# Three attention steps as one group, with one inserted piece, up to step 237

## The chip, the cores and the metric

The kernel runs on one core of a Trainium2 chip. The metric is the device time of one execution in microseconds. The profile is of one execution; its times are counted from the first instruction of the program.

## The reference

Two kinds of layer follow each other, twice: multi-head attention with a residual, then Fourier mixing (FNet) with a residual, each on a layer-normalised input. The sequence has 2048 rows of 640 columns; there are 32 heads of 20 columns.

```python
def _A_ref(x, wqkv, wo):
    qkv = (x @ wqkv).reshape(B, S, 3, H, Dh) ...
    scores = einsum("bhqd,bhkd->bhqk", q, k) * (Dh ** -0.5)
    o = einsum("bhqk,bhkd->bhqd", softmax(scores), v)
    return o.reshape(B, S, D) @ wo

x = x + _A_ref(_layernorm(x), A_wqkv, A_wo)
x = x + _B_ref(_layernorm(x), ...)      # real part of a two-sided DFT
x = x + _A_ref(_layernorm(x), A_wqkv, A_wo)
x = x + _B_ref(_layernorm(x), ...)
```

## The kernel before

Each of the two layers has four stages: a prologue (loading, normalising, transposing, and the q, k and v of the first heads), attention, the output projection, and the Fourier stage. The change lies in attention.

**Steps.** Attention goes through 512 steps. A step is a group of four heads (`g`, eight of them), a block of 512 queries (`qb`, four) and a block of 128 keys (`kc`, sixteen); `kc` runs innermost. `scores(n, j)` (L477) makes one *score tile* of step n, two heads, j = 0 or 1: two matmuls (L483) into one of three PSUM tiles of two banks each, `p0` to `p2`, taken in turn, and the exp of it on ScalarE (L486) into one of seven SBUF tiles `e0` to `e6`, also in turn. So a score tile can be written only when the exp of the tile three before it has read its PSUM tile, and an exp only when the values have read the tile seven before. `values(n)` (L488) multiplies the four heads' exps of a step with v: four matmuls (L494), each of them two records in the profile, into the accumulator `acc`, one PSUM bank that collects sixteen steps. Then `finish` (L499) transposes it out on VectorE (L501), divides, transposes back, splits it in two parts and stores them with eight DMAs on GpSimd's queue (L515).

**Inserted work.** The q, k and v of the later heads are computed between the steps. `work` (L347) is a generator of *pieces*. A q or k block of 512 columns is a product of fifteen matmuls of 512 columns (L127, tile `pqk`), cut in a piece of eight and one of seven; after the second, `keep` (L209) copies, splits and squares it on VectorE and stores it. Two steps later `after` (L361) makes the *norm product* (L227, tile `pn`), whose maximum VectorE takes (L228). A v block is fifteen matmuls of 320 columns (tile `pv`), again eight and seven. All pieces and norm products share one PSUM bank, `fill`. `due` (L561) says how many pieces should be done by a step, from the marks of L559 (80 at step `THIN`); `need` (L598) forces them where the next head group wants them. In the first layer `compare` (L587) also hands out VectorE work step by step that tests whether the DFT matrices are mirrored (class `Check`, tiles `cq`, `far`).

**Order.** The program is written in the order in which each engine is to work, and that order stands; only semaphores are added. `sweep` (L518) is that order: at each step `begin` (key bounds, tasks, forced pieces), the loads of the next queries and keys on SyncE's queue (L446 to L464), both score tiles, then `between` (L626: `fill`, a piece or a norm product, and then up to two comparisons), then values. Up to step `THIN` = 236 a step with a piece does no values and the next step does all that are owed, so that values go two steps at a time next to pieces and one at a time elsewhere. After it values go one step at a time, or two to catch up after a piece.

`general` (L634) repeats the sweep for inputs whose bound is too loose; it is not taken here.

Of the kernel before, what the change touches and what calls it, by code (L numbers as in the profile page):

```python
# [35 lines left out]
def mha_fnet_kernel(ctx, tc, x_in, wqk, wv, wo, seq, hid, nat_seq, nat_hid, out):  # L36
# [123 lines left out]
    class Qkv:  # L160
# [256 lines left out]


    class Attention:
        THIN = 236  # L420

        def __init__(s, qkv, L):
            s.a = qkv
# [64 lines left out]
        def values(s, n):  # L488
            g, qb, kc = s.steps[n]
            if kc == 0:  # L490
                s.acc = bank("acc", [128, 512], "acc")
            for j in range(4):
                v0 = (4 * g + j) * VW
                PE.matmul(s.acc[32 * j:32 * j + 32], s.a.v[kc][:, v0:v0 + 32], s.e[n, j // 2][:, j % 2],  # L494
                          start=kc == 0, stop=kc == NT - 1, skip_group_check=True)
            if kc == NT - 1:
                s.finish(g, qb)

        def finish(s, g, qb):  # L499
            t0 = s.room("ofsh", [16, 32], F32, "of")  # L500
            V.transpose(t0.rearrange("p b c -> p (b c)"), s.acc)  # L501
            rc = const.tile([128, 16], F32, name="rc", bufs=2)
            V.tensor_scalar(rc, t0[:, :, DH], 1e-30, None, op0=OP.max)
            V.reciprocal(rc, rc)
# [10 lines left out]
                    G.dma_start(s.o[k, h * DH:(h + 1) * DH, qb * 512:(qb + 1) * 512],  # L515
                                hl[k][32 * j:32 * j + DH])

        def sweep(s, shift, begin, fill):  # L518
            done = calm = 0
            for n, (g, qb, kc) in enumerate(s.steps):  # L520
                begin(n, g, qb, kc)
                last = qb == NB - 1
                if kc == (7 if last else 10 if g == LATE else 4) and not (last and g == H // 4 - 1):
                    s.qload(*((g, qb + 1) if not last else (g + 1, 0)), shift)
                if last and g + 1 < H // 4:
                    for f, j in {1: [(0, 0)], 9: [(0, 1)], 11: [(1, 0)]}.get(kc, []):
                        s.kload(g + 1, f, j)
                if qb == 0 and kc == 0 and g:
                    s.kload(g, 1, 1)
                s.scores(n, 0)  # L530
                s.scores(n, 1)

                more, owed = fill(n) and n >= 2 and n + 1 < len(s.steps), n - 1 - done
                if n < s.THIN:
                    if more and kc != 1:
                        continue
                    count = owed
                else:  # L540
                    if more and owed < 3:
                        calm = n + 6
                        continue
                    count = min(owed, 1)
                    if owed > 1 and (done + 1) % NT and n >= calm:
                        calm = n + 6
                        count = 2
                for _ in range(count):
                    s.values(done)
                    done += 1  # L550
            for n in range(done, len(s.steps)):
                s.values(n)

        def run(s, done, project, check):

# [31 lines left out]
            def compare(n):  # L587

                for _ in range(2):
# [8 lines left out]
            def need(n, *keys):  # L598
                while not all(k in s.a.made for k in keys):
                    if s.after:  # L600
                        fill(s.after[0])
# [29 lines left out]
            s.sweep("b", begin, between)  # L631
            assert not s.work and not later and not tasks, (len(later), len(tasks))

        def general(s, project):  # L634

            f = nc.values_load(s.a.flag[0:1, 0:1], min_val=0, max_val=1)
            with tc.If(f < 1):
# [30 lines left out]
                s.sweep("m", lambda *_: None, lambda *_: None)  # L668
                for f in sum(project.early.values(), []):
                    f()  # L670

# [685 lines left out]
```

## Time and profile before

| what | value |
|---|---|
| median of three runs | 2623.97 us (2621.59 to 2625.21) |
| profiled execution, its own time | 2620.62 us |
| its span, first to last instruction | 2618.8 us |
| first attention, 97.1 to 1149.9 us | 1052.8 us |
| second attention, 1408.3 to 2453.5 us | 1045.2 us |
| exps, one of 128x1024 | 2048, mean 1115 ns with overlap |
| value matmuls (records) | 8192, busy 1062.4 us |
| score matmuls | 4096, busy 815.6 us |

A row of a timeline gives the start, the time from the first start to the last end, the engine, the line and operation, output and input tile, and the number of instructions merged in the row; in brackets stands the idle time before it and what ended it. Starts are measured; ends of matmuls are modelled, and consecutive matmuls overlap. A row of stretches gives the length and the busy time of each engine with the number of its instructions, then the granted TensorE clock, and the DMA share and rate. PE is TensorE's matmuls, PEld its weight loads, DVE is VectorE, ACT ScalarE, POOL GpSimd, SP SyncE.

### The profile page before, as it was taken

The numbers are of one execution on the slowest core, as the hardware profiler recorded it, in microseconds if no ns is written. First come the engines' busy times: TensorE is split into PE (matmuls) and PEld (weight loads), VectorE is DVE, ScalarE is ACT, GpSimd is POOL, SyncE is SP. The second block draws the span as 40 slices with busy tenths as digits, with TensorE's granted clock in tenths as the row PEclk, the third lists the DMA queues.
The fourth block names the chain that finished last, engine by engine and source line by source line (L and its number), as shares of the span: only waits on it lengthen the run. The fifth ranks groups of instructions, "written<-read, shape, count | busy, mean of one in ns | idle before, by whom it ended". The sixth has DMA issues, their size and how long they took to land. (4 is left out here: it accounts for less than half of the span.)

```text
span 2618.8 us, 43736 instructions
## 1 busy us (share of the span) xinstructions
PE 2524.8 (96%) x16350; PEld 1162.1 (44%) x16350; DVE 981.4 (37%) x2079; ACT 2137.4 (82%) x2429; POOL 528.6 (20%) x1068
## 2 busy tenths in 40 slices
PE   7999999999999999999879999999999999999998
PEld 6643444443333332248666444444433333322586
DVE  5355533455444434416652333111321212121265
ACT  5588899988999999964245888999899999999652
POOL 2122111222221122213420111111111111211233
PEclk9999999999999999999989999999999999999998
DMA  4244322333333223326442232111121212132364
GB/s 165 97 127 133 107 94 76 104 99 114 116 112 104 82 60 102 108 83 231 175 175 81 79 100 68 55 28 60 62 73 55 74 41 65 49 89 91 112 232 156
DMA packets 124942, 264.05 MB, mean 101 GB/s; under 512 B 28080, under 2 KB 52432, under 8 KB 124700
## 3 DMA queue, kind: packets, MB, share of 16 engines
q1 hardware_dynamic: 83804, 150.61, 17.5%
q0 software_dynamic: 40896, 110.34, 13.3%
q8 instruction: 137, 2.24, 0.4%
q14 instruction: 105, 0.86, 0.1%
HBM read 176.60 MB, written 84.21 MB: 100 GB/s over the span
## 5 line engine op out<-in xcount | busy, mean ns | idle before, releaser
L486 ACT ACTIVATE e<-psc 128x1024 f32<-128x1024 f32 x2048 | 1938.3, 1115 | 162.9 <-PE psc L483 122.1
L494 PE MATMUL acc<-e,v 128*32 128x512 f32 x8192 | 1062.4, 602 | 7.0 <-DVE of L501 6.4
L483 PE MATMUL psc<-stq,stk 62*128 62x512 f32 x4096 | 815.6, 463 | 3.0 <-ACT e L486 3.0
L483 PEld LDWEIGHTS psc<-stq,stk 62*128 62x128 f32 x4096 | 341.4, 184 | 836.0 <-ACT e L486 781.0
L494 PEld LDWEIGHTS acc<-e,v 128*32 128x32 f32 x8192 | 187.6, 108 | 369.3 <-issue 338.6
L515 POOL DMA_DIRECT2D o<-oh x256 | 131.0, 519 | 941.0 <-DVE oh L510 939.0
L127 PE MATMUL pqk<-xt,wqk 128*128 128x512 f32 x1200 | 314.1, 405 | 6.6 <-DVE top L228 4.8
L127 PEld LDWEIGHTS pqk<-xt,wqk 128*128 128x128 f32 x1200 | 215.4, 188 | 91.3 <-issue 37.9
L501 DVE STREAM_TRANSPOSE of<-acc 128x512 f32<-128x512 f32 x64 | 45.9, 717 | 527.3 <-PE acc L494 527.3
L112 DVE CAST hl<-pqk 128x512 fp32r<-128x512 f32 x64 | 44.2, 691 | 423.2 <-PE pqk L127 419.2
L127 PE MATMUL pv<-wv,xt 128*128 128x320 f32 x960 | 161.3, 318 | 4.3 <-DVE hl L220 4.1
L127 PEld LDWEIGHTS pv<-wv,xt 128*128 128x128 f32 x960 | 142.1, 189 | 31.6 <-issue 24.5
L515 POOL DMA_DIRECT2D o<-ot x256 | 128.3, 508 | 0.7 <-issue 0.4
L120 PE MATMUL py<-wo,o 128*128 128x320 f32 x320 | 100.5, 314 | 14.4 <-DVE xr L904 7.6
L222 POOL DMA_DIRECT2D scrq<-hl x40 | 28.4, 710 | 385.6 <-DVE hl L115 263.7
L721 DVE TENSOR_REDUCE far<-cq 128x1 f32<-128x512 f32 (+5 forms) x169 | 98.6, 584 | 5.7
L121 PE MATMUL py<-wo,o 128*128 128x320 f32 x320 | 99.5, 311 | 0.0
L122 PE MATMUL py<-wo,o 128*128 128x320 f32 x320 | 99.4, 311 | 0.0
L725 DVE TENSOR_TENSOR cq<-cq 128x512 f32<-128x512 f32 (+4 forms) x166 | 96.5, 581 | 3.3 <-DMA cq<-in_nat_seq_dram 3.0
L258 DVE COPY v<-pv 128x320 f32<-128x320 f32 x32 | 15.7, 490 | 182.1 <-PE pv L127 182.1
L222 POOL DMA_DIRECT2D scrk<-hl x40 | 28.1, 702 | 272.4 <-DVE hl L115 244.0
L716 POOL DMA_DIRECT2D cq<-in_nat_seq_dram x64 | 46.3, 729 | 129.5 <-DVE far L721 107.7
(191 smaller groups left out, 1755.7 us busy)
## 6 DMA issues: line engine op xcount, KB each, us to landing
cq<-in_nat_seq_dram POOLq DMA_DIRECT2D x64, 512.0 KB, 5.6
scrq<-hl POOLq DMA_DIRECT2D x40, 512.0 KB, 3.2
scrk<-hl POOLq DMA_DIRECT2D x40, 512.0 KB, 3.4
stq<-scrq SPq DMA_DIRECT2D x256, 80.0 KB
stk<-scrk SPq DMA_DIRECT2D x128, 160.0 KB
o<-o SPq DMA_DIRECT2D x16, 1280.0 KB
stq<-scrq SPq DMA_DIRECT2D x256, 40.0 KB
stk<-scrk SPq DMA_DIRECT2D x128, 80.0 KB
```

The source lines that it names most:

```text
L120: PE.matmul(out_ap, ah, bh, start=start, stop=False)
L121: PE.matmul(out_ap, ah, bl, start=False, stop=False)
L122: PE.matmul(out_ap, al, bh, start=False, stop=stop)
L127: yield lambda i=i, j=j, k=k: PE.matmul(out_ap, a[i], b[j], start=dc == 0 and k == 0, stop=dc == ND - 1 and k == 2)
L222: G.dma_start(s.scr["qk"[k]][c * 128:(c + 1) * 128, :, tb * 512:(tb + 1) * 512], hl.bitcast(F32))
L483: PE.matmul(p[:, i], s.k[g, kc // 8, j][r, kc % 8 * 128:(kc % 8 + 1) * 128], s.q[g, qb, j][r], start=True, stop=True)
L486: A.activation(e, p, AF.Exp, scale=SCALE)
L494: PE.matmul(s.acc[32 * j:32 * j + 32], s.a.v[kc][:, v0:v0 + 32], s.e[n, j // 2][:, j % 2], start=kc == 0, stop=kc == NT - 1, skip_group_ch ...
L515: G.dma_start(s.o[k, h * DH:(h + 1) * DH, qb * 512:(qb + 1) * 512], hl[k][32 * j:32 * j + DH])
L716: G.dma_start(t, quarters[i])
L721: V.tensor_reduce(to, x, op=OP.max, axis=AX.X, apply_absolute_value=True)
L725: V.tensor_tensor(y, x, y, op=op)
```

## The change

Up to step `THIN`, now 237, three steps go together. Scores are still issued in the order of steps. A piece, where one is due, stands between the two score tiles of the steps with `kc` 2, 5, 8, 11 and 15, and behind both of step 13 (there only if no block is half done). Values of all steps before the present one are done in one run behind the scores of the steps with `kc` 0, 3, 6, 9, 12 and 13: three steps each time, and one at 13. The norm product of a block, and up to three comparisons, come behind a value run (`close`). `finish` becomes a generator: its first transpose is issued with the last values, its remainder behind the run and, up to step 237, behind the norm product and the comparisons. After a block's last chunk a pause of four steps is kept where new weights were split. The bound of the next head group and its first key load come one step later. After step 237 the rule for values is what it was, but comparisons now come behind the values and the rest of `finish` instead of before them.

```diff
@@ work()
                             if i + 1 < len(order):
+                                s.pause = 4 if i != 3 else 0
                                 w[i + 1] = s.weights(...)
...
-        THIN = 236
+        THIN = 237
...
             if kc == NT - 1:
-                s.finish(g, qb)
+                s.tail = s.finish(g, qb)
+                next(s.tail)
 
         def finish(s, g, qb):
             t0 = s.room("ofsh", [16, 32], F32, "of")
             V.transpose(t0.rearrange("p b c -> p (b c)"), s.acc)
+            yield
...
-        def sweep(s, shift, begin, fill):
-            done = calm = 0
+        def sweep(s, shift, begin, fill, close):
+            done, calm, s.tail = 0, 0, ()
...
-                    for f, j in {1: [(0, 0)], 9: [(0, 1)], 11: [(1, 0)]}.get(kc, []):
+                    for f, j in {2: [(0, 0)], 9: [(0, 1)], 11: [(1, 0)]}.get(kc, []):
...
                 s.scores(n, 0)
+                if n < s.THIN and kc in (2, 5, 8, 11, NT - 1):
+                    fill(n)
                 s.scores(n, 1)
-                more, owed = fill(n) and n >= 2 and n + 1 < len(s.steps), n - 1 - done
                 if n < s.THIN:
-                    if more and kc != 1:
-                        continue
-                    count = owed
+                    if kc == 13:
+                        fill(n)
+                    if kc in (0, 3, 6, 9, 12, 13):
+                        while done < n:
+                            s.values(done)
+                            done += 1
+                        close(n, 3)
+                        list(s.tail)
+                    continue
+
+                owed = n - 1 - done
+                if fill(n) and owed < 3 and n + 1 < len(s.steps):
+                    calm = n + 6
                 else:
-                    if more and owed < 3:
-                        calm = n + 6
-                        continue
-                    count = min(owed, 1)
-                    if owed > 1 and (done + 1) % NT and n >= calm:
-                        calm = n + 6
-                        count = 2
-                for _ in range(count):
-                    s.values(done)
-                    done += 1
+                    count = 2 if owed > 1 and n >= calm and (done + 1) % NT else min(owed, 1)
+                    if count == 2:
+                        calm = n + 6
+                    for _ in range(count):
+                        s.values(done)
+                        done += 1
+                    list(s.tail)
+                close(n, 2)
...
-                    s.after = (n + 2, f) if f and not s.more else None
-                    s.rest = n + 4 if s.after else n
+                    s.after = (n + (1 if n < s.THIN else 2), f) if f and not s.more else None
+                    s.rest = n + (2 if n < s.THIN or not s.after else 4)
...
+            def after(n):
+                if s.after and n >= s.after[0]:
+                    f, s.after, s.a.pause = s.after[1], None, 0
+                    f()
+                    s.rest = max(s.rest, n + s.a.pause)
+
             def fill(n):
-                if s.after:
-                    if n >= s.after[0]:
-                        f, s.after = s.after[1], None
-                        f()
-                elif s.work and n >= s.rest and (s.more and n < s.THIN or s.blocks < due(n + 1)):
+                if n >= s.THIN:
+                    if s.after:
+                        return after(n)
+                elif s.after or s.more and n % NT == 13:
+                    return
+                if s.work and n >= s.rest and (s.more and n < s.THIN or s.blocks < due(n + 1)):
                     block(n)
-                    s.rest = max(s.rest, n + 2)
                     return s.work
...
-                    when, to = 0, g + 1
+                    when, to = 1, g + 1
...
-            def between(n):
-                more = fill(n)
-                compare(n)
-                return more
+            def close(n, count):
+                if n < s.THIN:
+                    after(n)
+                compare(n, count)
```

More of the change, by code (lines that the diff above doesn't have):

```diff
@@ L530, in sweep @@
                 s.scores(n, 0)
+                if n < s.THIN and kc in (2, 5, 8, 11, NT - 1):
+                    fill(n)
                 s.scores(n, 1)
-                more, owed = fill(n) and n >= 2 and n + 1 < len(s.steps), n - 1 - done
                 if n < s.THIN:
-                    if more and kc != 1:
-                        continue
-                    count = owed
-                else:
-                    if more and owed < 3:
+                    if kc == 13:
[10 more added lines that the diff above has]
+                    calm = n + 6
+                else:
+                    count = 2 if owed > 1 and n >= calm and (done + 1) % NT else min(owed, 1)
+                    if count == 2:
                         calm = n + 6
-                        continue
-                    count = min(owed, 1)
-                    if owed > 1 and (done + 1) % NT and n >= calm:
-                        calm = n + 6
-                        count = 2
-                for _ in range(count):
-                    s.values(done)
-                    done += 1
+                    for _ in range(count):
[3 more added lines that the diff above has]
+                close(n, 2)
             for n in range(done, len(s.steps)):
                 s.values(n)
+            list(s.tail)
         def run(s, done, project, check):
@@ L575, in block, with compare @@
                     tasks.extend(done())
-            def fill(n):
-                if s.after:
-                    if n >= s.after[0]:
-                        f, s.after = s.after[1], None
-                        f()
-                elif s.work and n >= s.rest and (s.more and n < s.THIN or s.blocks < due(n + 1)):
+            def after(n):
[3 more added lines that the diff above has]
+                    s.rest = max(s.rest, n + s.a.pause)
+            def fill(n):
+                if n >= s.THIN:
[4 more added lines that the diff above has]
+                if s.work and n >= s.rest and (s.more and n < s.THIN or s.blocks < due(n + 1)):
                     block(n)
-                    s.rest = max(s.rest, n + 2)
                     return s.work
-            def compare(n):
-                for _ in range(2):
+            def compare(n, count):
+                for _ in range(count):
                     if not later or n < s.landed or (len(check) - len(later)) * 490 >= n * len(check):
@@ L600, in need @@
                     if s.after:
-                        fill(s.after[0])
+                        after(s.after[0])
                     else:
@@ L624, in begin @@
                     f()
-            def between(n):
-                more = fill(n)
-                compare(n)
-                return more
-            s.sweep("b", begin, between)
+            def close(n, count):
+                if n < s.THIN:
+                    after(n)
+                compare(n, count)
+            s.sweep("b", begin, fill, close)
             assert not s.work and not later and not tasks, (len(later), len(tasks))
@@ L667, in general @@
                 s.qload(0, 0, "m")
-                s.sweep("m", lambda *_: None, lambda *_: None)
+                s.sweep("m", lambda *_: None, lambda n: None, lambda *_: None)
                 for f in sum(project.early.values(), []):
```

## The prediction

> **What bounds the kernel now.** I read the page first (busy time by engine, the 40 slices, the costliest groups), then the busy time of each engine over four stretches that I cut at the first score matmul of each attention, at step 237 and at its end, then the order in which TensorE, ScalarE and VectorE start their work inside two short windows. The chain of waits is of little use here: it follows TensorE almost throughout. From the page:
>
> ```profile
> PE 2524.8 (96%) x16350; PEld 1162.1 (44%) x16350; DVE 981.4 (37%) x2079; ACT 2137.4 (82%) x2429; POOL 528.6 (20%) x1068
> ...
> L486 ACT ACTIVATE e<-psc 128x1024 f32<-128x1024 f32 x2048 | 1938.3, 1115 | 162.9 <-PE psc L483 122.1
> ...
> scrq<-hl POOLq DMA_DIRECT2D x40, 512.0 KB, 3.2
> ```
>
> From the stretches (columns: length, then busy time of PE, PEld, DVE, ACT, POOL); the first and third are steps 0 to 236 of the two attentions, and the same stretches for the score line alone show 948 matmuls, that is 237 steps of four:
>
> ```profile
> 97.10:625.65 528.55, 521.30 (x3453) 220.04 (x3452) 250.63 (x508) 459.38 (x475) 105.94 (x181) 1.00 0.34 107
> 625.65:1149.90 524.25, 518.68 (x3429) 165.01 (x3432) 217.17 (x511) 508.27 (x550) 116.45 (x209) 1.00 0.31 95
> 1408.30:1933.35 525.05, 520.91 (x3453) 219.89 (x3452) 136.25 (x250) 459.12 (x475) 75.45 (x140) 1.00 0.21 67
> 1933.35:2453.50 520.15, 517.48 (x3427) 164.78 (x3430) 104.38 (x214) 508.08 (x550) 77.60 (x150) 1.00 0.22 65
> ...
> 97.10:625.65 528.55, 174.24 (x948) 71.93 (x948) 1.00 0.34 107
> 1408.30:1933.35 525.05, 174.06 (x948) 71.79 (x948) 1.00 0.21 67
> ```
>
> The reader is to see two regimes. Up to step 237 TensorE is busy 99% of 528.55 and 525.05 us and ScalarE 87%: TensorE sets the pace. After it ScalarE is busy 97%. But 87% is little room: whatever lets TensorE run ahead meets ScalarE soon. And the granted clock is 1.00 in all four, so it plays no part. What the groups cost TensorE is read as the distance from one start to the next in its timeline (the ends are modelled and overlap):
>
> ```profile
> 303.19 0.73 PE L483 MATMUL psc<-stq,stk 62*128 62x512 f32 x4
> 303.85 0.39 PE L227 MATMUL pn<-sq,ind 128*32 128x512 bf16 x1
> 303.86 1.24 PE L494 MATMUL acc<-e,v 128*32 128x512 f32 x8
> 305.03 0.73 PE L483 MATMUL psc<-stq,stk 62*128 62x512 f32 x4
> ...
> 307.41 2.14 PE L127 MATMUL pqk<-xt,wqk 128*128 128x512 f32 x8
> 309.47 0.73 PE L483 MATMUL psc<-stq,stk 62*128 62x512 f32 x4
> 310.13 1.92 PE L494 MATMUL acc<-e,v 128*32 128x512 f32 x16
> 311.99 0.73 PE L483 MATMUL psc<-stq,stk 62*128 62x512 f32 x4
> 312.65 1.88 PE L127 MATMUL pqk<-xt,wqk 128*128 128x512 f32 x7
> 314.46 0.73 PE L483 MATMUL psc<-stq,stk 62*128 62x512 f32 x4
> ...
> 319.48 1.06 PE L494 MATMUL acc<-e,v 128*32 128x512 f32 x8
> 320.47 0.73 PE L483 MATMUL psc<-stq,stk 62*128 62x512 f32 x4
> 321.13 1.44 PE L127 MATMUL pv<-wv,xt 128*128 128x320 f32 x8
> 322.50 0.74 PE L483 MATMUL psc<-stq,stk 62*128 62x512 f32 x4
> 323.17 1.92 PE L494 MATMUL acc<-e,v 128*32 128x512 f32 x16
> 325.02 0.73 PE L483 MATMUL psc<-stq,stk 62*128 62x512 f32 x4
> 325.69 1.29 PE L127 MATMUL pv<-wv,xt 128*128 128x320 f32 x7
> 326.90 0.74 PE L483 MATMUL psc<-stq,stk 62*128 62x512 f32 x4
> ```
>
> So: scores of one step (two tiles) 0.66; a piece of a q/k block 2.06 (eight matmuls) or 1.81 (seven); of a v block 1.37 or 1.21; values of one step 0.99 (319.48 to 320.47) and of two together 1.86 (each instruction has two records, hence x8 and x16); a norm product 0.19 (1.18 for it and one step of values, less 0.99). I check these prices on the program as it is. Counted in its built order, steps 0 to 236 hold 235 score groups and one of two steps (2.04 from its rows), 76 single and 79 double value runs, 24 norm products, 24 + 24 q/k pieces, 16 + 16 v pieces: 155.1 + 2.0 + 75.2 + 146.9 + 4.6 + 92.8 + 41.3 = **517.9 us**. The stretches took 528.55 and 525.05, so 7 to 11 us are waits, and the prices hold.
>
> **What the change does to TensorE.** The built order of the changed kernel has the same 80 pieces before step 237, one norm product fewer (it comes later, 0.2), and otherwise other groups: 69 cycles of the form *three score tiles, piece, three score tiles, three steps of values*; four with six tiles and no piece; one at the start with five tiles, piece, three tiles; and 14 short groups *two tiles, (piece), one step of values*. Each three steps thus have two score groups and one value run in place of three and about two. The new prices: a third step of values adds 1.86 - 0.99 = 0.87, so 2.73 for three (bounds: 0.87 and 0.99 for that third). A third score tile is read from the window at the start of the first attention, the one place where before issues more than two in a row:
>
> ```profile
> 99.81 0.96 PE L483 MATMUL psc<-stq,stk 62*128 62x512 f32 x6
> 101.43 0.50 PE L483 MATMUL psc<-stq,stk 62*128 62x512 f32 x2 [0.65 <-ACT e L486]
> 101.85 1.89 PE L127 MATMUL pqk<-xt,wqk 128*128 128x512 f32 x7
> ...
> 100.35 3.77 ACT L486 ACTIVATE e<-psc 128x1024 f32<-128x1024 f32 x4 [0.73 <-PE psc L483]
> ```
>
> Six matmuls last 0.96 against 0.73 for four, so a tile adds 0.23 and three tiles cost 0.89. TensorE's work alone would then be 139 x 0.89 + 13.6 + 3.3 (the longer and the short score groups: 4 x 1.58, 1.35, 14 x 0.66 = 16.9) + 74 x 2.73 + 14 x 0.99 + 4.4 + 134.1 = **495 us**, 23 less per attention.
>
> **The wait that it adds.** The same four rows show it. There are three score banks. The fourth tile of that window (101.43) stood 0.65 us for ScalarE: it uses the bank of the first, whose exp began at 100.35, so a bank comes free 1.08 after its exp begins, and the tile that had to wait then takes 0.42 until the next group begins (unhindered the last tile of a group takes 0.33, half of 0.66). The pitch of exps is (3.77 - 1.03) / 3 = 0.913, with one exp's length and its start from:
>
> ```profile
> 324.33 1.02 ACT L486 ACTIVATE e<-psc 128x1024 f32<-128x1024 f32 x1 [0.19 <-PE acc L494]
> 325.62 2.91 ACT L486 ACTIVATE e<-psc 128x1024 f32<-128x1024 f32 x3 [0.27 <-PE psc L483]
> 328.73 1.03 ACT L486 ACTIVATE e<-psc 128x1024 f32<-128x1024 f32 x1 [0.19 <-PE acc L494]
> ```
>
> Scores issued at 325.02 have their exp at 325.62: 0.60. Now one new cycle, tiles A to F, from the start of A:
> - exp of A at 0.60, of C two pitches later, at 2.43.
> - F takes C's bank, free at 2.43 + 1.08 = 3.51. With the eight-matmul q/k piece F would be ready at 0.89 + 2.06 + 0.56 = 3.51, just in time; with 1.81, 1.37, 1.21 or no piece it is ready earlier and stands.
> - the values begin at 3.51 + 0.42 = 3.93, and TensorE is back at A after 3.93 + 2.73 = **6.66 us, whatever the piece**.
> - ScalarE does not run ahead meanwhile: its sixth exp begins at 0.60 + 5 x 0.913 = 5.17 and ends near 6.2, and the next A comes at 6.66, its exp at 7.26. It idles 1.2 us in each cycle, because TensorE, in order, cannot give it scores during 2.73 us of values. The ring of seven exp tiles does not add to this: F's exp waits for the first step of values, released 1.16 after a run begins (323.17 to 324.33), here at 5.09, before 5.17.
>
> Queued behind the waiting F is the value run, and the next scores behind that; who waits is ScalarE. For a rule of TensorEngine Tiling, Performance Considerations (PSUM Bottleneck), in the Trainium skill, that tiling speeds TensorE and not the emptying of PSUM, the trace agrees: by it a cycle stays at 6.66, and without it at TensorE's 5.7 to 6.6.
>
> Per attention: 73 x 6.66 = 486.2; the first cycle 8.7 (fifth tile at 0.60 + 0.913 + 1.08 = 2.59, then 0.42 + 2.06 + 0.89 + 2.73); the short groups 5 x (0.66 + 1.37 + 0.99) + 5 x (0.66 + 2.06 + 0.99) + 4 x 1.65 = 40.3; 23 x 0.19 = 4.4 for norm products. For VectorE I add 3: the norm's reduction now stands just before the next piece, in the one bank of pieces.
>
> ```profile
> 304.28 0.68 DVE L228 TENSOR_REDUCE top<-pn 32x1 f32<-32x512 f32 x1 [1.48 <-PE pn L227]
> ```
>
> It ends 1.11 after the norm (303.85) starts; the piece comes at 0.19 + 0.89 = 1.08 in a long cycle, at 0.85 in the four short ones. The bounds are 1 (no other VectorE work in front) and 12 (one more instruction of 0.68 in front of each of the 17 such pieces). The sum is **542.6 us**, against 528.55 and 525.05: +14.0 and +17.6. Before paid less in the stretches of v pieces: the two-step round 321.13 to 325.69 takes 4.56, 2.28 a step, next to rounds without a piece; 6.66 for three is 2.22 a step in all of them.
>
> **What else moves.** The transpose that frees the accumulator is now issued ahead of the rest of its step's VectorE work, and comparisons (three at each value run, two before at each step) behind it. After step 237 that can help the first attention, which takes 524.25 there against 520.15 in the second, which has no comparisons; I take -2 of these 4.1 (bounds -4 and +2: comparisons that fell behind are caught up there). The moved norm product costs 0.2 each time. The key load one step later, the bound's chain one step later and the output DMAs (same number, issued behind the values) have several steps of lead on SP's and POOL's queues: nothing, and without that cover one landing at each of the seven changes of head group, some 3.2 us by the page's store of a q block.
>
> Sum: 31.6 - 2 + 0.4 = +30. On the profiled execution's 2620.62 this is 2650.6; the median of the runs, 2623.97, lies 3.4 higher, which would give 2654. I forecast **2652 us**.
>
> **Rivals.** *Fewer switches pay.* If F found its bank free (exps keep up, or the 0.42 and 1.08 overlap the piece), the cycles would cost TensorE's work alone: 6.57, 6.32, 5.88, 5.72, and 5.48 (six exps) without a piece; 504.5 us per attention, -44.6 in all, **2578**. For it speaks the page's 96% of PE against 82% of ACT; against it the 0.65 us wait. It decides by whether F stands behind `ACT e`. The Trainium skill's TensorEngine Tiling, Tiling Modes (Key Properties), says a change of tiling mode drains TensorE, and would give this rival; the 0.99 against 0.87 for a step of values agrees in kind. *Half of it*: F stands half as long: 523.6, about **2616**. *Slower than before by more*: with comparisons issued three at a time, one pair (0.68 + 0.69, as below) stands in front of the reduction or of the piece's copies, and 17 pieces of the first attention wait 1.4 us each: +24, **2676**; it decides if the piece's start stands behind `DVE top`.
>
> ```profile
> 309.47 0.69 DVE L721 TENSOR_REDUCE ctop<-cq 128x1 f32<-128x512 f32 x1 [4.51 <-DMA cq<-in_nat_seq_dram]
> 310.07 0.68 DVE L725 TENSOR_TENSOR cq<-cq 128x512 f32<-128x512 f32 x1
> ```
>
> That the grouping does not happen is excluded by the built order.
>
> **How the numbers follow.** Forecast 0.80, switches pay 0.09, half 0.04, VectorE 0.07. The forecast's own bounds: F's 0.42 as 0.33 is -13; the third step of values as 0.99 is +18; VectorE and the part after step 237 -6 to +13; not all at the same end, 2634 to 2676, which takes in the VectorE case and leaves the two faster ones out. Faster by over 0.2% (about what a measurement of this kernel can tell) 0.11, within it 0.04, slower 0.85.
>
> **What would show it.** Steps 0 to 236 take 540 to 546 us in both attentions with ScalarE at 84% or less; three-step rounds last 6.6 to 6.7 us with every kind of piece, the v pieces too; the sixth tile's row names `ACT e`; ScalarE's idle time behind `PE psc` grows from 122 us. I am wrong if rounds with v pieces last under 6.2 us, or if the loss is found after step 237.

## The result: 1.55% slower, where 1.1% was forecast

| | before | after |
|---|---|---|
| median of four runs | 2622.78 us | 2662.70 us (2657.77 to 2666.54) |
| ratio, with its 95% interval | | 1.0155 (1.0129 to 1.0181) |
| span of the profiled execution | 2618.8 us | 2662.9 us |

The forecast was 2652 us, with a range of 2634 to 2676 and 0.85 on slower. The medians lie 40 us apart where the forecast had 28 (30 between executions); the two profiled executions lie 44.1 us apart. From the page of after, the busy time of the engines and the groups of exps and of score matmuls:

```profile
PE 2535.5 (95%) x16350; PEld 1196.7 (45%) x16350; DVE 979.7 (37%) x2079; ACT 2112.0 (79%) x2429; POOL 528.1 (20%) x1068
...
L490 ACT ACTIVATE e<-psc 128x1024 f32<-128x1024 f32 x2048 | 1912.9, 1121 | 233.8 <-PE psc L487 219.0
...
L487 PE MATMUL psc<-stq,stk 62*128 62x512 f32 x4096 | 826.9, 466 | 43.1 <-ACT e L490 37.9
```

The same exps are done, and ScalarE now waits 219.0 us for scores where it waited 122.1. At the same time the score matmuls stand 37.9 us for exps (3.0 before, by the grouped view). Each engine waits for the other more than it did. Where that is, the stretches of after say, cut as those of before (length, busy PE, PEld, DVE, ACT, POOL, then the granted clock):

```profile
97.98:653.30 555.32, 532.53 (x3460) 237.37 (x3460) 248.23 (x505) 446.15 (x474) 104.69 (x179) 0.98 0.31 100
653.30:1174.00 520.70, 516.92 (x3417) 165.70 (x3416) 218.30 (x514) 507.99 (x549) 116.42 (x209) 1.00 0.31 95
1433.20:1978.40 545.20, 522.87 (x3461) 234.23 (x3460) 133.36 (x244) 446.35 (x475) 75.33 (x139) 1.00 0.20 63
1978.40:2499.00 520.60, 517.01 (x3415) 165.60 (x3414) 106.68 (x220) 508.00 (x549) 78.17 (x151) 1.00 0.22 66
```

Against the rows of before, steps 0 to 236 cost 26.8 and 20.2 us more (555.32 for 528.55, 545.20 for 525.05), the first attention's remainder 3.5 less, the second's 0.5 more. So the place is the forecast one: ScalarE's share there falls to 80% and 82%, TensorE's busy time, whose ends are modelled, grows by 11.2 and 2.0, and the loss is in how the two take turns. A whole round with a v piece, with the end of the one before it and the start of the next, on TensorE; then the exps of it and of the one before it, on ScalarE:

```profile
344.33 0.83 PE L487 MATMUL psc<-stq,stk 62*128 62x512 f32 x4
345.58 0.50 PE L487 MATMUL psc<-stq,stk 62*128 62x512 f32 x2 [0.42 <-ACT e L490]
346.01 2.78 PE L498 MATMUL acc<-e,v 128*32 128x512 f32 x24
348.72 0.96 PE L487 MATMUL psc<-stq,stk 62*128 62x512 f32 x6
349.62 1.28 PE L127 MATMUL pv<-wv,xt 128*128 128x320 f32 x7
350.83 0.99 PE L487 MATMUL psc<-stq,stk 62*128 62x512 f32 x4
352.23 0.50 PE L487 MATMUL psc<-stq,stk 62*128 62x512 f32 x2 [0.42 <-ACT e L490]
352.66 2.78 PE L498 MATMUL acc<-e,v 128*32 128x512 f32 x24
355.37 0.73 PE L487 MATMUL psc<-stq,stk 62*128 62x512 f32 x4
```

```profile
342.67 5.61 ACT L490 ACTIVATE e<-psc 128x1024 f32<-128x1024 f32 x6 [1.25 <-PE psc L487]
349.32 5.61 ACT L490 ACTIVATE e<-psc 128x1024 f32<-128x1024 f32 x6 [1.05 <-PE psc L487]
```

The round runs from 348.72 to 355.37: 6.65 us. Its exps begin at 349.32, 0.60 after the scores; the sixth tile (352.23) stands for `ACT e`; the values run from 352.66, and ScalarE, which does six exps in 5.61, had idled 1.05 before it got these scores. This is the cycle that the prediction drew.

The mean rounds of the second attention, by kind, in us:

| round | count | predicted | measured |
|---|---|---|---|
| v piece of eight or of seven | 10 and 16 | 6.66 | 6.66 and 6.68 |
| q/k piece of seven | 24 | 6.66 | 6.58 |
| q/k piece of eight, no norm product | 5 | 6.66 | 6.72 |
| q/k or v piece of eight, with norm product | 13 and 1 | 6.85 | 7.09 and 6.96 |
| no piece (with norm product) | 1 (3) | 6.66 (6.85) | 6.89 (6.96, and one of 8.46) |
| the first one | 1 | 8.7 | 8.64 |
| short, with piece: v; q/k | 5; 1 | 3.02; 3.71 | 3.03; 3.71 |

The table cuts a round at its first matmul, the norm product included. A norm product begins 2.60 after the start of the value run before it, the next scores without one 2.71, so the 24 rounds with a q/k piece of seven, which all end at a norm product, count 0.11 short: to the next scores they last 6.69. Told without that cut, the time from a round's first scores to its values is 3.94 (the median) with every kind of piece, where the prediction had 3.93, and three steps of values take 2.71 where it had 2.73.

One thing was not in the forecast: 0.98 in the clock column of the first attention. Two neighbouring stretches of it, the first from the start of the scores of a round without a piece, the second its values, and the timeline of the same time:

```profile
280.60:285.00 4.40, 3.01 (x16) 1.28 (x12) 1.16 (x3) 4.40 (x5) 1.46 (x2) 0.87 0.51 135
285.00:290.40 5.40, 5.40 (x28) 1.01 (x26) 0.00 (x0) 2.11 (x3) 0.00 (x0) 0.50 0.71 239
```

```profile
281.56 0.50 PE L487 MATMUL psc<-stq,stk 62*128 62x512 f32 x2 [0.21 <-ACT e L490]
282.47 0.50 PE L487 MATMUL psc<-stq,stk 62*128 62x512 f32 x2 [0.41 <-ACT e L490]
283.39 0.56 PE L487 MATMUL psc<-stq,stk 62*128 62x512 f32 x2 [0.42 <-ACT e L490]
284.31 0.86 PE L487 MATMUL psc<-stq,stk 62*128 62x512 f32 x2 [0.35 <-ACT e L490]
285.10 5.35 PE L498 MATMUL acc<-e,v 128*32 128x512 f32 x24
290.38 1.08 PE L487 MATMUL psc<-stq,stk 62*128 62x512 f32 x6
```

Without a piece between them, four score tiles in a row wait for exps. Towards the end of these 4.4 us the granted clock falls (to 0.50, from 283.8 on, for 6.8 us), and the value run behind them takes 5.28 (285.10 to 290.38) instead of 2.72. There are five such groups in each attention, the first round (whose fourth and fifth tile wait, ahead of its piece) and the four rounds without a piece. In the first attention the low clock befell four of them, the first round among them, in the second attention one.

### The profile page after: what moved, and what is told of

Same layout as the page of the kernel before. It is cut to its first block, busy times and chain, and to the rows that moved or that the text cites. A ratio compares the mean times of both kernels' runs of the same rounds, so it can differ in the third digit from the quotient of the medians.

```text
span 2662.9 us, 43748 instructions
## 1 busy us (share of the span) xinstructions
PE 2535.5 (95%) x16350; PEld 1196.7 (45%) x16350; DVE 979.7 (37%) x2079; ACT 2112.0 (79%) x2429; POOL 528.1 (20%) x1068
## 5 line engine op out<-in xcount | busy, mean ns | idle before, releaser
L490 ACT ACTIVATE e<-psc 128x1024 f32<-128x1024 f32 x2048 | 1912.9, 1121 | 233.8 <-PE psc L487 219.0
L498 PE MATMUL acc<-e,v 128*32 128x512 f32 x8192 | 1032.9, 604 | 2.3 <-DVE of L506 1.8
L487 PE MATMUL psc<-stq,stk 62*128 62x512 f32 x4096 | 826.9, 466 | 43.1 <-ACT e L490 37.9
L487 PEld LDWEIGHTS psc<-stq,stk 62*128 62x128 f32 x4096 | 359.2, 184 | 821.9 <-ACT e L490 635.4
L498 PEld LDWEIGHTS acc<-e,v 128*32 128x32 f32 x8192 | 198.2, 109 | 397.9 <-issue 380.6
L736 POOL DMA_DIRECT2D cq<-in_nat_seq_dram x64 | 46.9, 735 | 166.5 <-DVE far L741 135.5
```

The lines of the kernel that those rows point to most:

```text
L487: PE.matmul(p[:, i], s.k[g, kc // 8, j][r, kc % 8 * 128:(kc % 8 + 1) * 128], s.q[g, qb, j][r], start=True, stop=True)
L490: A.activation(e, p, AF.Exp, scale=SCALE)
L736: G.dma_start(t, quarters[i])
```

## Experiments

Four theories stood against each other for the loss. *Bank*: the forecast's cycle, in which the sixth tile waits for a PSUM bank and the long value run for the sixth tile. *Work*: TensorE itself does more or slower work (mode switches, loads of the queries). *Clock*: the excess over the forecast is the low clock in groups without a piece. *Stretch*: what the change loses, it loses next to v pieces, where before paid 2.28 us a step.

**e1, fill the waits.** Matmuls that nobody reads stand where a three-step group has no piece: eight of them, and four in the first group.

```diff
                 if n < s.THIN and kc in (2, 5, 8, 11, NT - 1):
+                    was = s.blocks
                     fill(n)
+                    if shift == "b" and s.blocks == was:
+                        s.idle(8)
+                if n == 1 and shift == "b":
+                    s.idle(4)
```

> The changed kernel, with eight idle matmuls in each group of six score tiles that has no piece, and four behind the third tile of the first group; their product is read by nobody. Clock theory: in the changed kernel these groups leave TensorE mostly waiting for 4.3 us, the granted clock then falls to 0.50 for 3.4 or 6.8 us, and the value run behind takes up to 5.3 us instead of 2.71. With the idle matmuls the clock stays at 1.00 up to step 237, and the six places give back 2.6 + 1.5 + 2.9 + 2.4 us in the first attention and 1.5 in the second: about 11 us less than the changed kernel, some 2651 us; steps 0 to 236 take 546 and 544 us instead of 555.3 and 545.2. Rival: these value runs are slow because the query loads run at the same time (239 GB/s in that stretch); then nothing changes, 2662 us, and the runs still last 4 to 5.3 us.

Median 2656.48 us, ratio to before 1.0125 (1.0109 to 1.0142); the profiled span is 7.5 us shorter than after's. Steps 0 to 236 of the two attentions, and the TensorE timeline around a filled group:

```profile
97.80:645.27 547.47, 529.94 (x3497) 241.24 (x3497) 248.34 (x505) 446.25 (x474) 104.66 (x179) 1.00 0.32 102
...
1426.94:1971.06 544.12, 528.24 (x3497) 239.92 (x3496) 133.34 (x244) 446.68 (x475) 75.33 (x139) 1.00 0.20 63
```

```profile
277.76 2.11 PE L528 MATMUL idle<-xt 128*128 128x512 f32 x8
279.80 0.96 PE L487 MATMUL psc<-stq,stk 62*128 62x512 f32 x6
280.70 2.78 PE L498 MATMUL acc<-e,v 128*32 128x512 f32 x24
283.41 0.97 PE L487 MATMUL psc<-stq,stk 62*128 62x512 f32 x6
```

More work, less time: the value run is back at 2.71 (280.70 to 283.41), the filled rounds last 6.96 to 7.01, but for one of 7.23 and one of 8.38, and the first one 8.73 and 8.65. The first attention gains 7.9 us, the second, which had one low-clock round, 1.1. The DMAs move 348 GB/s during that very run (239 in the stretch of after's), so the rival, that query loads slow these runs, falls and the clock theory holds. The medians differ by 6 us where 11 were expected. One short fall of the clock is left in the steps, at 586.9, behind a wait for VectorE (below); it lies in the round of 8.38.

**e2, give the values back in two runs.** The first two steps of values go ahead of the sixth score tile, the third behind it.

```diff
+                if n < s.THIN and kc in (0, 3, 6, 9, 12):
+                    while done < n - 1:
+                        s.values(done)
+                        done += 1
                 s.scores(n, 1)
```

> The changed kernel, with the value run of three steps split: two steps of values, the sixth score tile, then one step of values. Bank theory: the sixth tile no longer stands for its bank, and ScalarE gets a tile in the middle of the run; a round with a v piece costs 0.89 + 1.37 or 1.21 + 0.66 + 1.86 + 0.43 + 0.99 = 6.2 or 6.0 us instead of 6.66, one with a q/k piece 6.6 or 6.9 instead of 6.6 or 6.75, and the rounds without a piece leave TensorE waiting less, so that the clock falls less often. In all 10 to 30 us less than the changed kernel, 2632 to 2652 us. Rival, switches: each of the 74 rounds of an attention has two groups more at 0.33 us for both, 49 us more in all, about 2711 us.

2649.91 us, ratio 1.0102 (1.0085 to 1.0119), 13 us under after. TensorE has more groups to change between, and yet a round is over sooner; one round with a v piece of eight in the second attention:

```profile
1661.71 0.96 PE L487 MATMUL psc<-stq,stk 62*128 62x512 f32 x6
1662.60 1.43 PE L127 MATMUL pv<-wv,xt 128*128 128x320 f32 x8
1663.97 0.84 PE L487 MATMUL psc<-stq,stk 62*128 62x512 f32 x4
1664.73 1.92 PE L498 MATMUL acc<-e,v 128*32 128x512 f32 x16
1666.59 0.51 PE L487 MATMUL psc<-stq,stk 62*128 62x512 f32 x2
1667.02 1.06 PE L498 MATMUL acc<-e,v 128*32 128x512 f32 x8
1668.02 0.96 PE L487 MATMUL psc<-stq,stk 62*128 62x512 f32 x6
```

From 1661.71 to 1668.02 are 6.31 us in place of 6.66: the sixth tile no longer stands, since its bank comes free while two steps of values run. What remains in this round is work. Rounds with a v piece of seven last 6.30, not the 6.0 that was expected: there the fifth tile still waits a little, and the two kinds come out alike again. That speaks for the bank and against the theory that changes between groups are what costs.

**e3 and e10, a slower ScalarE.** If the bank sets the round, a longer pitch of exps lengthens every round alike. e3 puts one copy of a single column behind each exp of steps 0 to 236, e10 two copies that do not depend on each other (shown).

```diff
             A.activation(e, p, AF.Exp, scale=SCALE)
+            if n < s.THIN and s.short:
+                for x in (zero, one):
+                    A.activation(x, x, AF.Copy)
```

> The changed kernel, with a one-column copy on ScalarE behind each exp before step 237. Its price is bounded by 0.19 us (the accumulator read of before) and 0.39 us (a two-column activation of before). Bank theory: the sixth tile waits for the third exp, two pitches behind the first, so each three-step round grows by two prices, 0.4 to 0.8 us, and 73 rounds of each attention by 28 to 57 us: 2719 to 2776 us, rounds at 7.0 to 7.4 us with every kind of piece. Rival: TensorE's own work sets the 6.66 us (runs of three cost more than their rows say); ScalarE idles 1.2 us in a round, six copies take that up or little more, and the time grows by less than 0.1 us a round at the lower price, under 2677 us.

e3 took 2682.61 us in its one run, far under what the bank theory was expected to give and 6 us above the bound of its rival. The copy is what was mis-sized: it overlaps the exp, and the pitch went only from 0.905 to 0.997. For that pitch the bank's rule (twice the pitch, less the 0.06 by which the first exp then began earlier) gives +0.12 a round, and the rounds grew from 6.66 and 6.68 to 6.78 and 6.80. It agrees, but by too little to settle anything.

> The changed kernel, with two one-column copies to two different places behind each exp before step 237 (in e6_act2 the second waited for the first and the pitch became 1.24, beyond what ScalarE's idle time can take up under either theory). Pitch about 1.09. Bank theory: rounds of 0.55 + 2 x 1.09 + 1.07 + 0.43 + 2.72 = 6.95 us, 2695 to 2710 us. Rival: six exps take 6.5 us, less than a round, so rounds stay at 6.7 to 6.8 us, 2663 to 2680 us.

e10: 2715.23 us, steps 0 to 236 575.7 and 573.1. The pitch is 1.09. The wait of the sixth tile, in a round with a q/k piece of seven in the second attention:

```profile
1698.88 0.97 PE L488 MATMUL psc<-stq,stk 62*128 62x512 f32 x6
1699.78 1.88 PE L127 MATMUL pqk<-xt,wqk 128*128 128x512 f32 x7
1701.59 0.73 PE L488 MATMUL psc<-stq,stk 62*128 62x512 f32 x4
1702.69 0.50 PE L488 MATMUL psc<-stq,stk 62*128 62x512 f32 x2 [0.37 <-ACT e L491]
1703.12 2.78 PE L502 MATMUL acc<-e,v 128*32 128x512 f32 x24
```

Rounds of the second attention last 6.91 with a q/k piece of seven (7.02 to the next scores), 6.98 and 6.96 with v pieces of seven and eight, 7.08 with a q/k piece of eight: again nearly the same whatever the piece, 0.3 to 0.4 longer, near the 6.95 that the bank predicts; TensorE's work, unchanged, would have left the long pieces at 6.7 to 6.8. From the first scores to the values it is 4.24 (the median) with every kind of piece, where the bank's sum is 0.55 + 2 x 1.09 + 1.07 + 0.43 = 4.23 and after has 3.94. This also settles the piece of eight q/k matmuls, for which the prediction's sums of work (6.57) and of the bank (6.66) lie too close to be told apart. The total is 5 us above the expected 2695 to 2710, and the low clock accounts for about that much: the first group took 11.51 us, a group without a piece 10.36.

**e6, the same with two copies that depend on each other.**

> The changed kernel, with two one-column copies on ScalarE behind each exp before step 237. One such copy raised the pitch of exps from 0.905 to 0.997 and the rounds from 6.66 to 6.78 us, and shortened the time from scores to the first exp by 0.06. Bank theory: two pitches lie before the sixth tile, so two copies give 0.905 + 2 x 0.092 and rounds of 6.66 + 2 x 0.184 - 0.06 = 6.97 us, about 23 us more per attention than the changed kernel: 2700 to 2712 us. Rival, TensorE's own work sets the round: six pitches grow by 1.1 us in all, which ScalarE's idle 1.2 us of a round takes up, and rounds stay at 6.8 us, 2680 us.

2771.6 us. The second copy waited for the first, the pitch became 1.238, and six exps (7.4 us) then fill the whole round of 7.2 to 7.5: ScalarE itself is the bound, which neither theory had. Inconclusive.

**e4 and e7, the old order in a part of the steps.** e4 restores the two-step order for steps 98 to 191; e7 exactly as long as v pieces are handed out (its edit is the one shown).

```diff
+                was, zone = zone, s.a.vnow and n < s.THIN
...
+                if zone or was:
+                    if not zone or not fill(n) or kc == 1:
+                        while done < n - zone:
+                            s.values(done)
+                            done += 1
+                        list(s.tail)
+                    close(n, 2)
+                    continue
```

> The changed kernel, with the old two-step order (a piece behind a step's scores, no values in that step) for steps 98 to 191 alone, where the v pieces lie. Bank theory: the loss lies in the rounds with short pieces; steps 96 to 191 take 200 to 203 us as before instead of 219.6, in both attentions, some 35 us less than the changed kernel: about 2627 us, close to the kernel before. Rival: grouping costs everywhere alike (20 to 27 us over 237 steps), so that 94 of them give back 40%, about 18 us: 2644 us.

e4: 2636.53 us, ratio 1.0047 (1.0030 to 1.0064). Steps 96 to 191 took 206.9 us in both attentions, against 219.6 in after and 200.6 in before, so between the two expectations. Most of the difference to before is not in the order of the rounds: the changed kernel hands its pieces out at other steps, and those 96 steps hold 30 q/k matmuls where before's hold 15, which is one block more (2.06 + 1.81), three norm products (3 x 0.19) and one step of values (0.99); before's 200.6 and these make 206.0. Equal steps are not equal work here.

> The changed kernel, with the old two-step order exactly while v pieces are inserted, and grouping by three for all q/k pieces (in e4_zone four pieces of two q/k blocks fell into the two-step stretch, where the kernel before has two). Bank theory: a pair of v pieces costs 4.55 us for two steps and steps without a piece 1.66 to 1.82, against 6.66 for three steps; a v block and its six steps then cost 12.6 against 13.3 plus the short groups, 16 blocks save 13 to 16 us per attention, and the kernel takes 2630 to 2637 us. Rival, grouping costs alike with every piece: as e4_zone or worse, 2637 to 2645 us.

e7: 2633.05 us, ratio 1.0040 (1.0026 to 1.0055), within what was expected. Steps 0 to 236:

```profile
96.73:631.68 534.95, 522.13 (x3462) 229.15 (x3462) 248.56 (x505) 451.18 (x474) 103.84 (x179) 0.99 0.33 104
...
1409.43:1943.18 533.75, 521.61 (x3461) 228.86 (x3461) 133.04 (x244) 451.70 (x475) 75.04 (x139) 0.99 0.21 65
```

With the same matmuls in steps 96 to 191 as after (30 of q/k, 240 of v, two norm products) it takes 204.8 us there, after 219.6: grouping costs 14.8 us in this stretch alone. Before's 200.6 and the block and norm products more that e7 does there (3.9 + 2 x 0.19 = 4.3) make 204.9, so the old order explains the stretch to 0.1 us. Outside it e7 gains another 5.6 us in the first attention and gives 3.3 back in the second; both meet the low clock in other places (0.99), and what e7 still loses against before lies there and, by difference, next to q/k pieces and in the groups without a piece.

**e5, only the accumulator's transpose first.** The kernel before, with nothing changed but `finish` split behind its transpose, and comparisons and the rest of `finish` behind the values.

```diff
             if kc == NT - 1:
-                s.finish(g, qb)
+                s.tail = s.finish(g, qb)
+                next(s.tail)
...
                     done += 1
+                list(s.tail)
+                close(n)
```

> The kernel before, with one part of the change alone: the rest of finish and the comparisons are issued behind the values of a step, as in the changed kernel after step 237; the grouping of steps is the old one. If the order of VectorE's work is what took the part after step 237 of the first attention from 523.8 to 520.4 us in the changed kernel, that part takes 520 to 521 us here too, the second attention is unchanged (525.0 and 519.6), and the kernel takes 3 to 4 us less than before, about 2619 us. If the gain came from pieces or comparisons that had been done at another time, nothing changes, 2622 us.

2619.82 us against 2623.39, ratio 0.9984 (0.9972 to 0.9995): better than both kernels, though the interval all but touches no change. Steps 237 on, in the first and the second attention:

```profile
626.73:1146.90 520.17, 517.34 (x3425) 164.88 (x3424) 216.67 (x511) 507.61 (x548) 115.83 (x209) 1.00 0.31 95
...
1932.73:2452.30 519.57, 516.92 (x3421) 164.60 (x3420) 104.27 (x214) 507.51 (x549) 77.39 (x150) 1.00 0.22 65
```

The 524.25 of the first attention's remainder fall to the second's level, as in after (520.70). So the 3.5 us that after gains there are this part of the change, and not the grouping. The trace of before shows them in one place. Values there waited for the transpose that frees the accumulator, which stood on VectorE behind comparisons (the first row is TensorE's, the second VectorE's):

```profile
825.24 1.06 PE L494 MATMUL acc<-e,v 128*32 128x512 f32 x8 [2.93 <-DVE of L501]
...
824.48 0.70 DVE L501 STREAM_TRANSPOSE of<-acc 128x512 f32<-128x512 f32 x1
```

From the scores at 821.50 to those at 831.05 three steps take 9.55 us, where their six exps at a pitch of 0.905 take 5.4: by this estimate the one stall costs 4.1 us, all that the first attention's remainder was longer than the second's. The longest wait for that transpose in the first attention after step 237 is 0.3 us in e5 and in after, and 2.93 again in e11 below, which keeps the old order.

**e8, e9 and e11, a faster ScalarE.** What would grouping be worth if exps came faster? Exps of three columns in four, the last quarter set to one by GpSimd (e8) or once for all in exp tiles that keep their place (e9 on after, e11 on before); these kernels leave out a quarter of the softmax before step 237. The core of e8's edit:

```diff
+            if n < s.THIN and s.short:
+                A.activation(e[:, :, :384], p[:, :, :384], AF.Exp, scale=SCALE)
+                G.memset(e[:, :, 384:], 1.0)
```

> The changed kernel, with exps of three quarters of the columns before step 237 (GpSimd sets the rest to one; a quarter of the softmax is left out there). The pitch of exps falls from 0.905 to about 0.70. Bank theory: the third exp begins at 0.60 + 1.40 = 2.00, the sixth tile's bank is free at about 2.87, and it no longer stands or hardly so: rounds fall to TensorE's own price, 5.7 to 5.9 us with v pieces, 6.3 with seven q/k matmuls, 6.6 with eight (before a norm product), so that the times differ by piece; steps 0 to 236 take 505 to 515 us in the second attention instead of 545, and the kernel about 2600 us. Rival, TensorE's own work sets 6.66 us: rounds and times as in the changed kernel, 2655 to 2663 us.

> The changed kernel, with exps of three quarters of the columns before step 237, as in e8_short, but without GpSimd: the seven exp tiles stay in place there and their last quarter is set to one once, by VectorE (a quarter of the softmax is left out before step 237). Pitch of exps about 0.70, third exp 2.0 us after the scores, its bank free at about 2.9. Bank theory: rounds of 6.0 to 6.1 us with v pieces, 6.2 to 6.3 with seven q/k matmuls, 6.5 with eight; steps 0 to 236 take 505 to 515 us in each attention instead of 555 and 545, the kernel 2580 to 2610 us. Rival, TensorE's own work sets the rounds: 6.6 to 6.7 us and 2655 to 2663 us.

> The kernel before, with the same short exps as e9_short2 (a quarter of the softmax is left out before step 237). Its TensorE work before step 237 is 518 us per attention by the rows, and 7 to 11 us of its 528.6 and 525.0 are waits. Bank theory: it falls to some 515 to 520 us, little, while the changed kernel with short exps falls to 505 to 515: there the grouping is faster, so the saving on TensorE is real and the banks hide it. Rival, grouping costs TensorE more than it saves: the changed kernel stays behind this one with short exps too.

As totals all three say nothing about grouping: 2778.43, 3012.46 and 2849.85 us, far above what was expected. In e8 GpSimd wrote its quarter only when the transfers queued ahead of it let it, and values waited up to 9.3 us for it. In e9 and e11 values waited for the newest exps, 260 and 225 us of TensorE's time in all, in e8 not at all. So it goes with the tiles that keep their place, which e8 has not, and not with grouping, which e11 has not; why is open. From e9:

```profile
408.05 1.88 PE L127 MATMUL pqk<-xt,wqk 128*128 128x512 f32 x7
409.86 0.96 PE L488 MATMUL psc<-stq,stk 62*128 62x512 f32 x6
412.73 3.70 PE L507 MATMUL acc<-e,v 128*32 128x512 f32 x20 [1.91 <-ACT e L496]
```

One thing can be read from them. At e8's pitch of 0.70 its undisturbed rounds last 6.03 with v pieces, 6.19 (6.30 to the next scores) and 6.53 with q/k pieces of seven and eight, so no longer the same for all. The v pieces are still at the bank (0.62 + 2 x 0.70 + 0.87 + 0.43 + 2.71 = 6.03, with the steps measured in e8), the q/k pieces near the prediction's sums of work, 6.32 and 6.57. And in e9 above, at 409.86, all three tiles behind a q/k piece go in one row without a wait for a bank. That is the bank theory's other side, seen in some rounds. What the whole kernel would gain stays open.

## Why the prediction was right, and where its sizes were off

- **That three steps go at the pace of the bank ring, 6.66 us whatever the piece: right.** It is the loss. TensorE's work alone would have made the rounds 5.5 to 6.6; they came at 6.66 to 6.72, and the sizes held as well as the path (3.94 from scores to values for 3.93, 2.71 for 2.73). e2 frees the sixth tile and the round falls by 0.35; e10 slows only ScalarE and every kind of round grows by 0.3 to 0.4. So the rivals "fewer switches pay" and "half of it" fall by the row they were to be decided by.
- **That v pieces no longer pay less: right,** 14.8 us of each attention's loss by e7.
- **"the granted clock is 1.00 in all four, so it plays no part": this step failed.** It read the clock of the old program into the new one, and read that one from means over some 525 us. Before had one fall itself, behind the 2.93 us wait above: 0.50 for 3.4 us from 826.79 on, which the mean of 1.00 does not show.

```profile
825.24:831.05 5.81, 5.81 (x33) 1.36 (x34) 4.97 (x10) 3.88 (x4) 3.14 (x7) 0.71 0.14 32
```

  In before score matmuls stand 3.0 us for exps in the whole run; the change makes ten groups (five in each attention) in which up to four tiles in a row stand for exps, and five of them met the low clock. The rounds of these five took 11.27, 8.50, 9.76, 9.39 and 8.46 where the same kinds take 8.64, 6.96, 6.89, 6.96 and 6.96: together 11.0 us, of which e1's profiled execution gives back 7.5 net, its own extra matmuls included. For this reason above all the first attention's 555.3 missed the 540 to 546 that the prediction named as a sign; the second's 545.2 lies within.
- **VectorE, 3 us per attention: right in size, and the rival of 24 did not come.** Comparisons did hold TensorE up once, not at a piece as the rival had it but at a norm product. At 583.9, in the first attention, comparisons and the rest of `finish` stood ahead of `keep` on VectorE, and the norm product behind them waited 1.72 us. The round took 8.44, 1.9 too long, and in its wake came one of the five low clocks:

```profile
592.38 0.38 PE L227 MATMUL pn<-sq,ind 128*32 128x512 bf16 x1 [1.72 <-DVE sq L216]
```

  The wait that the rival was to be known by, a piece behind `DVE top`, comes equally in both attentions, so it is not the comparisons but the reduction itself:

```profile
1510.07 2.12 PE L127 MATMUL pqk<-xt,wqk 128*128 128x512 f32 x8 [0.31 <-DVE top L228]
```

  It lengthens six of the thirteen long rounds with a norm product and a q/k piece (about 4.2 from scores to values for 3.94) and the four short ones (2.88 for 2.71): 6 x 0.27 + 4 x 0.17 = 2.3 us per attention where 3 were forecast. The norm product itself costs 0.20 (0.31 to the next scores, less the 0.11 by which it begins sooner), where 0.19 was forecast.
- **After step 237: -2 forecast, -3.5 measured,** shown by e5 to be the order around `finish`. The mechanism was right, and the 4.1 of which the term took a half go almost whole, since by the trace they were one stall.

So the first attention's 555.3 is 542.6 as forecast, 9.5 low clock, 1.9 the VectorE wait and 1.3 left over; the second's 545.2 is 542.6, 1.5 low clock and 1.1 left over. Of the 44.1 us between the two spans 46.9 lie in these two stretches (31.6 were forecast there), -3.1 in the attentions' remainders, and 0.3 outside attention. The excess over the forecast is for the most part the clock.

## What to carry to other kernels

Before grouping work on one engine, lay the ring of buffers between it and the next engine over the new order, tile by tile: a longer group that needs one more buffer than there is waits for the consumer, and then lets the consumer starve. A full share of busy time (96% here) does not say that saved work becomes saved time, if the other engine sits at 87% behind a ring of three. Where a change opens new waits on TensorE, price the clock in those waits too: a mean clock of 1.00 over a long stretch of the old program says nothing of them, and can hide a fall of its own.

## What the runs showed of the hardware

- The granted clock of TensorE fell although no single wait in that round was longer than 0.42 us: at 283.8, after three waits of 0.21 to 0.42 in 3.2 us, and it stayed at 0.50 for 6.8 us. The stretches at 0.50 inside the steps last 3.4 or 6.8 us. In the Trainium skill, TensorE: Matmul & The Clock Gate, Part 1 (A second HAM failure mode: psum-queue depth-cycling) says of another kernel that short idles between groups of matmuls that go round PSUM banks make the clock swing between half and full, and Part 1 (What's actually happening) gives 3413 ns for the window of activity; the trace agrees with both (0.50, 3.4 us). Which of the ten groups it hits the runs do not settle: rounds of one kind ran once at full clock and once not.
- One longer wait stood before a fall too: 2.93 us in before (825.24) and, in e5, 2.28 us of a piece for VectorE (293.06) were each followed within 2 us by 3.4 us at 0.50.
- A copy of one column on ScalarE behind an exp costs 0.09 us if nothing depends on it (pitch 0.905 to 0.997, with two 1.09), though its own record lasts about 0.2; two that depend on each other cost 0.33.
- The norm product costs TensorE the same at both places: 0.19 us between scores and values (before), 0.20 between values and scores (after).
